# Softmax mixing and a cosine feed-forward layer on one core: the two correction products of the first product take bf16 operands

## The chip, the core and the metric

The kernel runs on one core of a Trainium2 chip. The core's engines run side by side and meet through semaphores: TensorE (PE in the profile; PEld is its weight loads), VectorE (DVE), ScalarE (ACT), GpSimd (POOL) and SyncE (SP), which issues the transfers. The metric is the device time of one launch in microseconds (us), as a median over runs.

## The reference

```python
# _attn_ref: x (8, 4096, 192), weight_gen (8, 4096, 8 heads, 7 taps)
w = weight_gen - np.max(weight_gen, axis=-1, keepdims=True)
w = np.exp(w)
w = w / (np.sum(w, axis=-1, keepdims=True) + 1e-09)
x_unf = x_pad[:, idx, :].reshape(B, S, K, H, group)     # each row and the 6 before it
out = np.einsum('bshk,bskhg->bshg', w, x_unf)
# _moe_ref: w_in (192, 2048), w_out (2048, 192)
h = x @ w_in
g = h * np.cos(h)
return (g @ w_out).astype(np.float32)
```

Each of the 32768 rows is first a softmax-weighted mix of itself and the six rows before it, for eight heads of 24 columns. The mixed rows go through a product with `w_in` (192 to 2048), the function h cos h, and a product with `w_out` (2048 to 192). The weights arrive as 64-bit floats.

## The kernel before, in words

**Blocks and periods.** The rows are cut into 64 blocks of 512 (4 rows on each of 128 partitions). A block passes the feed-forward layer in 8 periods, one for each pair of 128-column chunks of `w_in`. Period i works on block i // 8 and pair i % 8, so there are 512 periods, and 7 more to drain. The Python loop over i writes every engine's instructions in order, and a last pass ties each engine to this order; nothing reorders them but the hardware.

**The first product** is done three times in float32r (`F32R`, a shortened float32 on TensorE) so that it comes out nearly as float32: a value is split into a high part, rounded to float32r, and a low part, what the rounding left. With `w` and `x` split in this way, the kernel adds low x times high w, high x times low w, and high x times high w. The first two are the correction products. The 192 input columns don't fill 128 partitions evenly, so matmuls use 64 partitions each, two side by side on the halves of the array ("64*128" in the profile). `ffn_in_first` issues three such pairs of matmuls of 512 columns, `ffn_in_second` six: nine pairs a period, into the two PSUM banks of tile `h`, of which there are three in turn. `wa_*` and `wb_*` hold `w_in` (`wb_*` the middle 64 input columns); `x_hi` and `x_lo` hold the transposed rows of a block.

**Between the two parts** stands `ffn_out(j)` for j = i - 6, the second product: 16 matmuls of high g times `wo` (high and low part of `w_out` side by side, 384 columns, float32r), two small transposes of rows of a block two ahead into spare columns of the same PSUM tile `acc`, and 16 matmuls of low g times a bf16 copy `wo_b` (192 columns). A float32r matmul brings its weight load with it; a bf16 one has a separate LDWEIGHTS.

**The chain for h cos h** runs over ACT and DVE: turns (ACT, line 369: h rounded to whole turns), fraction (DVE, 379), cosine (ACT, 383), g (DVE, 386), high g (ACT, 393), low g (DVE, 397). ACT's order within a period is: turns of i - 1, high g of i - 2, cosine of i - 1, then in every second period the copy of `acc` to SBUF (`part`, 450) and in the others the copy of the transposed rows to `x_hi` (301). The first product of period i + 3 needs the PSUM tile that low g of i gives free.

**POOL** computes the mixing of a block ahead (lines 261 and 276), the sums of the second product's halves (466, 467) and `x_lo` (303) from `part` and `x_hi`. Once in 32 periods a softmax of four blocks runs; its exponential on ACT needs another function table than the cosine, so two table loads stand around it, and POOL has the sums and products of this softmax (185 to 226). In what follows, the stretch around it is called the softmax stretch.

**The start.** Weights are converted while the first periods run: ACT, three steps on DVE, a high copy on ACT, the low part on POOL (`two_parts`, lines 124 to 150). `two_parts` can also write a bf16 copy of the value (`half`), which before only `w_out_2` asks for. Blocks 0 to 3 are transposed whole, into an `h` tile; the others row by row in `ffn_out`.

Of the kernel before, what the change touches and what calls it, by code (L numbers as in the profile page):

```python
# [12 lines left out]
F32R = mybir.dt.float32r  # L13
I32 = mybir.dt.int32
U16 = mybir.dt.uint16
BF16 = mybir.dt.bfloat16
# [4 lines left out]
P = 128  # L21
# [22 lines left out]
def tile_softmax_conv_then_cos_ffn(  # L44
# [8 lines left out]
    nc = tc.nc  # L53
# [5 lines left out]
    F = w_in.shape[1]  # L59
# [4 lines left out]
    CT = R * P  # L64
# [12 lines left out]
    const = ctx.enter_context(tc.tile_pool(name="const", bufs=1))  # L77
    gpool = ctx.enter_context(tc.tile_pool(name="gpool", bufs=9))
    work = ctx.enter_context(tc.tile_pool(name="work", bufs=2))
# [3 lines left out]
    def h_banks(k):  # L83

        return ps_h.tile([P, 2, CT], F32, name="h", tag=f"h{k % 3}", bufs=1)
# [11 lines left out]


    wa_hi = const.tile([P, F], F32R, name="wa_hi")
    wa_lo = const.tile([P, F], F32R, name="wa_lo")  # L100

    wb_hi = const.tile([P, F // 2], F32R, name="wb_hi")
    wb_lo = const.tile([P, F // 2], F32R, name="wb_lo")
    wo = const.tile([P, NFC, 2 * D], F32R, name="wo")
    wo_b = const.tile([P, NFC, D], BF16, name="wo_b")

    def words(n, home="ghi"):

        if home == "ghi":
            raw = gpool.tile([P, 2 * CW], I32, name="raw", tag=home)  # L110
        elif home == "fin":
            raw = work.tile([P, R * D], I32, name="raw", tag=home)
        else:
            raw = work.tile([P, 2 * CT], I32, name="raw", tag=home)
        return raw[:, 0:2 * n]
# [8 lines left out]
    def two_parts(raw, hi, lo, half=None):  # L124
        shape = hi.shape[1:]
        n = math.prod(shape)

        def shaped(t, steps):
            t = t.rearrange("p (n s) -> p n s", s=steps)
            return t if len(shape) == 1 else t.rearrange("p (a b) s -> p a b s", b=shape[1])  # L130

        low, top = (shaped(raw, 2)[..., k] for k in range(2))
        size, bits = (shaped(t[:, 0:n], 1)[..., 0] for t in room.pop(0))
        nc.scalar.activation(out=size.bitcast(F32), in_=top.bitcast(F32), func=AF.Abs, scale=F64_SCALE)
        yield
        nc.vector.tensor_scalar(  # L136
            out=size, in0=size, scalar1=3, scalar2=None, op0=ALU.logical_shift_left)
        yield

        nc.vector.scalar_tensor_tensor(  # L140
            out=size, in0=top, scalar=-0x80000000, in1=size, op0=ALU.bitwise_and, op1=ALU.bitwise_or)
        yield

        nc.vector.scalar_tensor_tensor(  # L144
            out=bits, in0=low, scalar=29, in1=size, op0=ALU.logical_shift_right, op1=ALU.bitwise_or)
        yield
        nc.scalar.copy(out=hi, in_=bits.bitcast(F32))
        if half is not None:
            nc.scalar.copy(out=half, in_=bits.bitcast(F32))
        nc.gpsimd.tensor_tensor(out=lo, in0=bits.bitcast(F32), in1=hi.bitcast(F32), op=ALU.subtract)  # L150

    def w_in_a(c0, c1, home="ghi"):
        raw = words(c1 - c0, home)
        for n in range(2):
            nc.sync.dma_start(out=raw[n * D2:(n + 1) * D2],
                              in_=w_in[n * P:n * P + D2, c0:c1].bitcast(I32))
        return two_parts(raw, wa_hi[:, c0:c1], wa_lo[:, c0:c1])

    w_in_odd_even = w_in.rearrange("k (a n c) -> n k a c", n=2, c=P)

    def w_in_b(j):
        raw = words(CW)
        pairs = slice(j * CW // P, (j + 1) * CW // P)
        for n in range(2):
            nc.sync.dma_start(out=raw[n * D2:(n + 1) * D2].rearrange("k (a c) -> k a c", c=2 * P),
                              in_=w_in_odd_even[1 - n, D2:P, pairs, :].bitcast(I32))
        cols = slice(j * CW, (j + 1) * CW)
        return two_parts(raw, wb_hi[:, cols], wb_lo[:, cols])

    w_out_v = w_out.rearrange("(c p) d -> p c d", p=P)  # L170

# [111 lines left out]
    xT, transposed = {}, set()  # L283

    def traded(t):

        nc.sync.keepalive_nop([nc.sync.lower_ap(t)])
# [4 lines left out]
    def parts_of(b):  # L292
        if b not in xT:
            hi = work.tile([P, 2, CT], F32R, name="x_hi")
            lo = work.tile([P, 2, CT], F32R, name="x_lo")
            xT[b] = (hi, lo)
        return xT[b]

    def split(b, t, cs, eng):
        hi, lo = parts_of(b)  # L300
        nc.scalar.copy(out=hi[:, :, cs], in_=t)
        yield
        eng.tensor_tensor(
            out=lo[:, :, cs], in0=t, in1=hi[:, :, cs].bitcast(F32), op=ALU.subtract)

# [24 lines left out]
    def chunk(pair, n):  # L330
        return slice((2 * pair + n) * P, (2 * pair + n + 1) * P)

    def ffn_in_first(i, h=None):

        b, pair = divmod(i, NPAIR)
        x_hi, x_lo = xT[b]
        if h is None:
            h = h_banks(i)
        for m, (w, v) in enumerate(((wa_hi, x_lo), (wa_lo, x_hi), (wa_hi, x_hi))):
            for q in range(2):  # L340
                rs = slice(q * D2, (q + 1) * D2)
                nc.tensor.matmul(  # L342
                    h[:, q, :], lhsT=w[rs, chunk(pair, q)], rhs=v[rs, q, :],
                    start=(m == 0), stop=False, skip_group_check=True)
        hs[i] = h
        traded(h)

    def ffn_in_second(i):

        b, pair = divmod(i, NPAIR)  # L350
        x_hi, x_lo = xT[b]
        h = hs[i]
        prods = ((wa_hi, x_lo, 0), (wa_lo, x_hi, 0), (wb_hi, x_lo, 1), (wb_lo, x_hi, 1),
                 (wa_hi, x_hi, 0), (wb_hi, x_hi, 1))
        for m, (w, v, middle) in enumerate(prods):
            for q in range(2):
                rs = slice(q * D2, (q + 1) * D2)
                cs = slice(pair * P, (pair + 1) * P) if middle else chunk(pair, 1 - q)
                nc.tensor.matmul(  # L359
                    h[:, 1 - q, :], lhsT=w[rs, cs], rhs=v[rs, q ^ middle, :],  # L360
                    start=False, stop=(m == len(prods) - 1), skip_group_check=True)
# [77 lines left out]
    def evacuate(j):  # L439
# [9 lines left out]
        if WHOLE < bt < NB:  # L449
            nc.scalar.copy(out=part, in_=acc)  # L450
            r = group % R
            splits.append(split(bt, part[:, :, 2 * D:], slice(r * P, (r + 1) * P), nc.gpsimd))
        else:
            nc.scalar.copy(out=part[:, :, 0:2 * D], in_=acc[:, :, 0:2 * D])  # L454
# [70 lines left out]
    def all_of(*steps):  # L525
# [4 lines left out]

    late = [
        (-1, 1, w_in_a, (768, 1280)), (-1, 2, w_in_b, (1,)), (-1, 2, w_out_2, (0,)),
        (0, 3, w_in_a, (1280, 1792)), (0, 3, w_out_2, (1,)), (1, 4, w_out_2, (2, "part1")),
        (1, 4, w_out_2, (3, "part1")), (2, 5, w_in_a, (1792, 2048, "fin")),
        (2, 5, w_out_2, (4, "fin")), (4, 6, w_out_2, (5, "part1")), (4, 7, w_out_2, (6, "part1")),
        (5, 8, w_out_2, (7, "fin")),
# [19 lines left out]
    next(sm1)  # L556
    w_a0 = w_in_a(0, 256)
    w_b0 = w_in_b(0)
    load_rows(1)
    w_a1 = w_in_a(256, 768)  # L560
# [4 lines left out]
    def go_on(steps, n):  # L565
        for _ in range(n):
# [4 lines left out]
                      t=own_taps.rearrange("p (r h) k -> p r h k", h=H))  # L571
# [15 lines left out]
    go_on(w_a0, 3)  # L587
    go_on(w_b0, 3)
    first = split(0, tr, slice(0, CT), nc.vector)
    go_on(first, 1)  # L590
    all_of(w_a0, w_b0)
# [12 lines left out]
    for i in range(N + LAG + 1):  # L604
        b, pair = divmod(i, NPAIR)
# [22 lines left out]
        def products():  # L628
            if b < NB and pair == 0:
                assert b in transposed  # L630
            if whole is not None and j >= 0:

                ffn_out(j)
                ffn_in_first(i, whole)
            elif j >= N - HALF:
                if j == N - HALF:
                    last_half()
                return
            elif busy and EXP + 2 <= step <= EXP + 3:

                ffn_out(j, rest=False)
                ffn_in_first(i)
                ffn_out(j, rest=True)
            else:
                if i < N:
                    ffn_in_first(i, h_now if whole is None else whole)
                if j >= 0:
                    ffn_out(j)
            if i < N:
                ffn_in_second(i)  # L650
            if j in stores:
                stores.pop(j)()
            if j >= 0:
                evacuate(j)
# [15 lines left out]
        if whole is not None:  # L670
            t = work.tile([P, 2, CT], F32, name="part0", bufs=3)
            nc.scalar.copy(out=t, in_=whole)
            later.append(split(b + 1, t, slice(0, CT), nc.vector))
# [72 lines left out]
```

## Time and profile before

| what | value |
|---|---|
| median of 3 runs | 2257.45 us (2256.27 to 2257.81) |
| profiled execution, first to last instruction | 2256.1 us |
| PE busy | 2203.8 us (98%), 26496 matmuls |
| PE weight loads busy | 2009.9 us (89%) |
| DVE, ACT, POOL busy | 1922.0, 1886.0, 2001.4 us |
| mean granted TensorE clock | 0.993 |
| DMA | 47 GB/s on average |

The three runs lie 0.2 to 1.7 us above the profiled execution's span. The profile is one execution. "Busy" of PE counts from a matmul's start to its modelled end, so neighbours overlap, and the time that a matmul really holds the array is read from the distance between the starts of pairs. In a row of the timeline stand the start, the time covered, engine, line, operation, tile written and tiles read, count, and in brackets the idle time before it with the instruction that ended it. From about 150 us to 2200 us the periods repeat with 4.25 us, except in the softmax stretch.

### The profile page before, as it was taken

How to read it: one execution, taken by the hardware profiler on the slowest of the kernel's cores; microseconds unless marked ns; L12 is line 12 of the kernel's file. 1: busy time of each engine (PE TensorE's matmuls, PEld its weight loads, DVE VectorE, ACT ScalarE, POOL GpSimd, SP SyncE). 2: the span in 40 equal slices, each digit the busy share in tenths (PEclk: the TensorE clock that was granted, in tenths of full speed). 3: DMA queues.
4: the chain of work that ended last, by engine and by line, in shares of the span. 5: the costliest groups of instructions: out<-in, count | busy, mean ns of one | idle time of the engine just before them, and what ended most of it. 6: DMA issues, size and time to landing. Idle time of an engine off the chain costs nothing.

```text
span 2256.1 us, 60616 instructions
## 1 busy us (share of the span) xinstructions
PE 2203.8 (98%) x26496; PEld 2009.9 (89%) x26496; DVE 1922.0 (85%) x1663; ACT 1886.0 (84%) x2111; POOL 2001.4 (89%) x1460
## 2 busy tenths in 40 slices
PE   4899999999999999999999999999999999999998
PEld 2788889889999889999999988899999999899887
DVE  7888888888888888888888888888888888888887
ACT  4788888888888888888888888888888888888886
POOL 7999999998998989989998998989989899899941
PEclk8899999999999999999999999999999999999999
DMA  6221121121221221221211211211211211212100
GB/s 157 57 59 43 33 59 39 46 51 34 51 50 36 49 59 26 50 59 27 58 46 31 59 44 41 51 43 42 51 48 37 58 30 47 59 26 53 33 9 22
DMA packets 25767, 105.55 MB, mean 47 GB/s; under 512 B 2734, under 2 KB 6566, under 8 KB 25502
## 3 DMA queue, kind: packets, MB, share of 16 engines
q1 hardware_dynamic: 25502, 101.67, 18.4%
q8 instruction: 208, 3.41, 0.6%
q14 instruction: 57, 0.47, 0.1%
HBM read 76.50 MB, written 25.17 MB: 45 GB/s over the span
## 4 chain that ended last, share of the span: by engine, by line
PE 94%; DVE 2%; ACT 2%; POOL 1%; issue 1%; DMA 0%; SPq 0%; POOLq 0%; DVEq 0%; ACTq 0%
PE acc L427 45%; PE h L359 31%; PE h L342 16%; PE acc L321 1%; DVE glo L397 1%; ACT part L450 1%; ACT ghi L393 1%; POOL xa L276 1%; POOL pr L261 1%; PE h L491 0%; DVE turn L379 0%; DMA xt<-in_x_dram 0%; DVE h L140 0%; DVE h L136 0%; PE h L312 0%
## 5 line engine op out<-in xcount | busy, mean ns | idle before, releaser
L379 DVE TENSOR_TENSOR turn<-h,turn 128x1024 f32<-128x1024 f32 x512 | 625.5, 1222 | 281.2 <-ACT turn L369 281.2
L427 PE MATMUL acc<-wo,ghi 64*128 64x384 f32 x8112 | 807.2, 335 | 0.3 <-ACT part L454 0.3
L427 PEld LDWEIGHTS acc<-wo,ghi 64*128 64x128 f32 x8112 | 736.7, 185 | 35.9 <-ACT part L450 3.1
L276 POOL TENSOR_TENSOR xa<-xa,pr 128x768 f32<-128x768 f32 (+1 forms) x384 | 703.0, 1831 | 0.6
L383 ACT ACTIVATE turn<-turn 128x1024 f32<-128x1024 f32 x512 | 543.4, 1061 | 188.5 <-DVE turn L379 185.1
L386 DVE SCALAR_TENSOR_TENSOR h<-h,turn 128x1024 f32<-128x1024 f32 x512 | 631.0, 1233 | 20.3 <-ACT turn L383 20.3
L397 DVE TENSOR_TENSOR glo<-h,ghi 128x1024 bf16<-128x1024 f32 x512 | 622.5, 1216 | 2.7 <-ACT ghi L393 1.7
L369 ACT ACTIVATE turn<-h 128x1024 int32<-128x1024 f32 x497 | 510.2, 1027 | 125.5 <-PE h L359 118.6
L261 POOL TENSOR_TENSOR pr<-xt,taps 128x768 f32<-128x768 f32 (+1 forms) x384 | 589.5, 1536 | 11.9
L393 ACT CAST ghi<-h 128x1024 fp32r<-128x1024 f32 x512 | 518.0, 1012 | 14.2 <-DVE h L386 14.2
L427 PE MATMUL acc<-wo_b,glo 64*128 64x192 bf16 x8112 | 431.1, 243 | 0.0
L466 POOL TENSOR_TENSOR part<-part,part 128x768 f32<-128x768 f32 x126 | 234.3, 1859 | 157.2 <-ACT part L450 130.3
L427 PEld LDWEIGHTS <-glo 64*128 64x128 bf16 x8112 | 333.5, 94 | 23.0 <-issue 11.0
L359 PE MATMUL h<-x_lo,wa_hi 64*128 64x512 f32 x1024 | 253.0, 477 | 0.7
L450 ACT COPY part<-acc 128x1024 f32<-128x1024 f32 x240 | 239.6, 998 | 3.6 <-PE acc L427 3.6
L342 PE MATMUL h<-x_lo,wa_hi 64*128 64x512 f32 x1024 | 217.3, 407 | 20.5 <-DVE t L144 14.1
L359 PE MATMUL h<-x_lo,wb_hi 64*128 64x512 f32 x1024 | 211.8, 397 | 0.0
L342 PE MATMUL h<-x_hi,wa_lo 64*128 64x512 f32 x1024 | 210.1, 392 | 1.3 <-POOL wa_lo L150 1.3
L359 PE MATMUL h<-x_hi,wa_hi 64*128 64x512 f32 x1024 | 211.1, 395 | 0.0
L342 PE MATMUL h<-x_hi,wa_hi 64*128 64x512 f32 x1024 | 210.5, 393 | 0.0
L359 PE MATMUL h<-x_hi,wb_hi 64*128 64x512 f32 x1024 | 208.6, 390 | 0.0
L359 PE MATMUL h<-x_hi,wb_lo 64*128 64x512 f32 x1024 | 208.5, 390 | 0.0
(73 smaller groups left out, 2163.3 us busy)
## 6 DMA issues: line engine op xcount, KB each, us to landing
xt<-in_x_dram SPq DMA_DIRECT2D x62, 960.0 KB, 6.8
out_dram<-fin SPq DMA_DIRECT2D x63, 384.0 KB, 3.4
taps<-in_weight_gen_dram SPq DMA_DIRECT2D x15, 448.0 KB, 4.8
raw<-in_moe_w_out_dram SPq DMA_DIRECT2D x8, 384.0 KB, 4.2
raw<-in_moe_w_in_dram SPq DMA_DIRECT2D x10, 256.0 KB, 10.8
xt<-in_x_dram SPq DMA_DIRECT2D x1, 768.0 KB, 10.5
xt<-in_x_dram SPq DMA_DIRECT2D x1, 540.0 KB, 5.5
raw<-in_moe_w_in_dram SPq DMA_DIRECT2D x4, 128.0 KB, 4.6
```

Of the source, the lines that this page charges most:

```text
L261: eng.tensor_tensor(out=dst.rearrange("p r (h g) -> p r h g", h=H), in0=xt[:, k + ra:k + rb, :].rearrange("p r (h g) -> p r h g", h=H), in ...
L276: eng.tensor_tensor(out=acc if k < K else xa, in0=acc, in1=old[:, ra:rb], op=ALU.add)
L342: nc.tensor.matmul(h[:, q, :], lhsT=w[rs, chunk(pair, q)], rhs=v[rs, q, :], start=(m == 0), stop=False, skip_group_check=True)
L359: nc.tensor.matmul(h[:, 1 - q, :], lhsT=w[rs, cs], rhs=v[rs, q ^ middle, :], start=False, stop=(m == len(prods) - 1), skip_group_check=True)
L369: nc.scalar.activation(out=t.bitcast(I32), in_=hs[i], func=AF.Identity, bias=0.25, scale=1.0)
L379: nc.vector.tensor_tensor(out=t, in0=hs[i], in1=t.bitcast(I32), op=ALU.subtract)
L383: nc.scalar.activation(out=t, in_=t, func=AF.Sin, bias=SIN_BIAS, scale=SIN_SCALE)
L386: nc.vector.scalar_tensor_tensor(out=hs[i], in0=hs[i], scalar=TWO_PI, in1=turns.pop(i), op0=ALU.mult, op1=ALU.mult)
L393: nc.scalar.copy(out=hi, in_=hs[i])
L397: nc.vector.tensor_tensor(out=lo, in0=hs.pop(i), in1=hi.bitcast(F32), op=ALU.subtract)
L427: nc.tensor.matmul(to, lhsT=g[rs, n, t * P:(t + 1) * P], rhs=w[rs, fc, :], start=(lo == 0 and c == 0 and (whole or s == 0)), stop=(lo == 1 ...
L450: nc.scalar.copy(out=part, in_=acc)
```

## The change

Both low parts, `x_lo` and `wa_lo`/`wb_lo`, become bf16 tiles, and bf16 copies of the whole values are added: `x_b` of the transposed rows, `wa_b` and `wb_b` of `w_in`. The correction products then read bf16 on both sides: `x_lo` times `wa_b`, and `wa_lo` times `x_b`. The product of the high parts stays in float32r. The copies are made on ACT: `x_b` in `split`, behind the yield that follows `x_hi`, and `wa_b`/`wb_b` in `two_parts`. The tiles take as much SBUF as before.

```diff
-    wa_lo = const.tile([P, F], F32R, name="wa_lo")
+    wa_lo = const.tile([P, F], BF16, name="wa_lo")
+    wa_b = const.tile([P, F], BF16, name="wa_b")
-    wb_lo = const.tile([P, F // 2], F32R, name="wb_lo")
+    wb_lo = const.tile([P, F // 2], BF16, name="wb_lo")
+    wb_b = const.tile([P, F // 2], BF16, name="wb_b")
...
-        return two_parts(raw, wa_hi[:, c0:c1], wa_lo[:, c0:c1])
+        return two_parts(raw, wa_hi[:, c0:c1], wa_lo[:, c0:c1], wa_b[:, c0:c1])
...
-        return two_parts(raw, wb_hi[:, cols], wb_lo[:, cols])
+        return two_parts(raw, wb_hi[:, cols], wb_lo[:, cols], wb_b[:, cols])
...
     def parts_of(b):
         if b not in xT:
             hi = work.tile([P, 2, CT], F32R, name="x_hi")
-            lo = work.tile([P, 2, CT], F32R, name="x_lo")
-            xT[b] = (hi, lo)
+            half = work.tile([P, 2, CT], BF16, name="x_b")
+            lo = work.tile([P, 2, CT], BF16, name="x_lo")
+            xT[b] = (hi, half, lo)
...
     def split(b, t, cs, eng):
-        hi, lo = parts_of(b)
+        hi, half, lo = parts_of(b)
         nc.scalar.copy(out=hi[:, :, cs], in_=t)
         yield
+        nc.scalar.copy(out=half[:, :, cs], in_=t)
         eng.tensor_tensor(
             out=lo[:, :, cs], in0=t, in1=hi[:, :, cs].bitcast(F32), op=ALU.subtract)
...
-        for m, (w, v) in enumerate(((wa_hi, x_lo), (wa_lo, x_hi), (wa_hi, x_hi))):
+        for m, (w, v) in enumerate(((wa_b, x_lo), (wa_lo, x_b), (wa_hi, x_hi))):
...
-        prods = ((wa_hi, x_lo, 0), (wa_lo, x_hi, 0), (wb_hi, x_lo, 1), (wb_lo, x_hi, 1),
+        prods = ((wa_b, x_lo, 0), (wa_lo, x_b, 0), (wb_b, x_lo, 1), (wb_lo, x_b, 1),
                  (wa_hi, x_hi, 0), (wb_hi, x_hi, 1))
```

On PE, from the end of one period's second part through the next first part to the second product, there stood before:

```order
L359 MATMUL h<-x_hi,wa_hi 128x512 x2
L359 MATMUL h<-x_hi,wb_hi 128x512 x2
L342 MATMUL h<-x_lo,wa_hi 128x512 x2
L342 MATMUL h<-x_hi,wa_lo 128x512 x2
L342 MATMUL h<-x_hi,wa_hi 128x512 x2
L427 MATMUL acc<-wo,ghi 128x384 x16
```

and there stands now (lines are those of the changed file):

```order
L363 MATMUL h<-x_hi,wa_hi 128x512 x2
L363 MATMUL h<-x_hi,wb_hi 128x512 x2
L346 LDWEIGHTS wa_b
L346 MATMUL h<-x_lo,wa_b 128x512
L346 LDWEIGHTS wa_b
L346 MATMUL h<-x_lo,wa_b 128x512
L346 LDWEIGHTS wa_lo
L346 MATMUL h<-x_b,wa_lo 128x512
L346 LDWEIGHTS wa_lo
L346 MATMUL h<-x_b,wa_lo 128x512
L346 MATMUL h<-x_hi,wa_hi 128x512 x2
L431 MATMUL acc<-wo,ghi 128x384 x16
```

Two of the three pairs of the first part read bf16 and have loads of their own; in the second part it is four of six, and these four follow directly on the bf16 matmuls of the second product. No matmul changes its place.

On ACT, in the softmax stretch and the periods behind it, there stood before (`turn` stands for turns and cosine, `ghi` for high g):

```order
L301 CAST x_hi<-part_4583 128x2x128
L301 CAST x_hi<-part_4736 128x2x128
L369 ACTIVATE turn<-h 128x1024
L393 CAST ghi<-h 128x1024
L383 ACTIVATE turn<-turn 128x1024
L450 COPY part_4878<-acc 128x1024
L369 ACTIVATE turn<-h 128x1024
L393 CAST ghi<-h 128x1024
L383 ACTIVATE turn<-turn 128x1024
L301 CAST x_hi<-part_4878 128x2x128
L369 ACTIVATE turn<-h 128x1024
```

and there stands now:

```order
L304 CAST x_hi<-part_4625 128x2x128
L304 CAST x_hi<-part_4778 128x2x128
L306 CAST x_b<-part_4625 128x2x128
L306 CAST x_b<-part_4778 128x2x128
L373 ACTIVATE turn<-h 128x1024
L397 CAST ghi<-h 128x1024
L387 ACTIVATE turn<-turn 128x1024
L454 COPY part_4923<-acc 128x1024
L373 ACTIVATE turn<-h 128x1024
L397 CAST ghi<-h 128x1024
L387 ACTIVATE turn<-turn 128x1024
L304 CAST x_hi<-part_4923 128x2x128
```

Each copy to `x_hi` gets a second one to `x_b` behind it, ahead of the next period's turns; where two rows' copies had been put together, two are added. The order on DVE and POOL is the same as before.

On ACT at the start, from the transposed block 0 to the conversion of the third piece of `w_in` (line 134 is its first step), there stood before:

```order
L301 CAST x_hi<-h 128x1024
L147 CAST wa_hi<-t_173 128x256
L147 CAST wb_hi<-t_173 128x512
L134 ACTIVATE h<-raw 128x512
L147 CAST wa_hi<-t_207 128x512
```

and there stands now:

```order
L304 CAST x_hi<-h 128x1024
L149 CAST wa_hi<-t_175 128x256
L151 CAST wa_b<-t_175 128x256
L149 CAST wb_hi<-t_175 128x512
L151 CAST wb_b<-t_175 128x512
L306 CAST x_b<-h 128x1024
L136 ACTIVATE h<-raw 128x512
L149 CAST wa_hi<-t_213 128x512
```

Three copies now stand ahead of the conversion of the third piece.

More of the change, by code (lines that the diff above doesn't have):

```diff
@@ L335, in ffn_in_first @@
         b, pair = divmod(i, NPAIR)
-        x_hi, x_lo = xT[b]
+        x_hi, x_b, x_lo = xT[b]
         if h is None:
             h = h_banks(i)
-        for m, (w, v) in enumerate(((wa_hi, x_lo), (wa_lo, x_hi), (wa_hi, x_hi))):
+        for m, (w, v) in enumerate(((wa_b, x_lo), (wa_lo, x_b), (wa_hi, x_hi))):
             for q in range(2):
@@ L350, in ffn_in_second @@
         b, pair = divmod(i, NPAIR)
-        x_hi, x_lo = xT[b]
+        x_hi, x_b, x_lo = xT[b]
         h = hs[i]
-        prods = ((wa_hi, x_lo, 0), (wa_lo, x_hi, 0), (wb_hi, x_lo, 1), (wb_lo, x_hi, 1),
+        prods = ((wa_b, x_lo, 0), (wa_lo, x_b, 0), (wb_b, x_lo, 1), (wb_lo, x_b, 1),
                  (wa_hi, x_hi, 0), (wb_hi, x_hi, 1))
```

## The prediction

> **What bounds the kernel now.** I read the page's first and fourth part (who is busy, and which chain ended last), then the waits, then one period's timeline.
>
> ```profile
> PE 2203.8 (98%) x26496; PEld 2009.9 (89%) x26496; DVE 1922.0 (85%) x1663; ACT 1886.0 (84%) x2111; POOL 2001.4 (89%) x1460
> PE 94%; DVE 2%; ACT 2%; POOL 1%; issue 1%; DMA 0%; SPq 0%; POOLq 0%; DVEq 0%; ACTq 0%
> ACT turn L369 <- PE h L359: 118.6, 207, 1.3
> PE h L342 <- DVE glo L397: 1.7, 10, 0.3
> ```
>
> TensorE is on the last chain for 94% of the span and almost never waits; ACT waits for it in 207 of the periods. So a period lasts as long as its matmuls, and the question is how close the others follow. One period of PE:
>
> ```profile
> 1003.83 0.44 PE L342 MATMUL h<-x_lo,wa_hi 64*128 64x512 f32 x2
> ...
> 1004.53 1.61 PE L427 MATMUL acc<-wo,ghi 64*128 64x384 f32 x16
> 1005.94 0.26 PE L321 MATMUL acc<-ident,xa 64*128 64x64 f32 x2
> 1005.99 0.82 PE L427 MATMUL acc<-wo_b,glo 64*128 64x192 bf16 x15
> ...
> 1006.91 0.43 PE L359 MATMUL h<-x_hi,wa_lo 64*128 64x512 f32 x2
> ...
> 1007.85 0.43 PE L359 MATMUL h<-x_hi,wb_hi 64*128 64x512 f32 x2
> 1008.08 1.22 PE L427 MATMUL acc<-wo,ghi 64*128 64x384 f32 x11
> ```
>
> A float32r pair of 512 columns holds the array for 0.234 us: five from 1006.91 to 1008.08 (no first product follows here), and three from 1003.83 to 1004.53. The period: 3 x 0.234 + 1.41 (wo) + 0.05 (transposes) + 0.92 (wo_b and the second part's first pair) + 5 x 0.234 = 4.25 us.
>
> **The streams.** What a bf16 pair takes is read from `wo_b`, and the weight loads stand beside it:
>
> ```profile
> L427 PE MATMUL acc<-wo_b,glo 64*128 64x192 bf16 x8096 | 429.4, 243 | 0.0
> L427 PEld LDWEIGHTS acc<-wo,ghi 64*128 64x128 f32 x8096 | 734.0, 185 | 35.5 <-ACT part L450 3.1 <-POOL wo L150 0.7 <-issue 0.3
> L427 PEld LDWEIGHTS <-glo 64*128 64x128 bf16 x8096 | 332.3, 94 | 22.7 <-issue 10.7
> 37.92 0.63 PE L359 MATMUL h<-x_hi,wa_lo 64*128 64x512 f32 x2
> 39.63 0.63 PE L359 MATMUL h<-x_hi,wb_hi 64*128 64x512 f32 x2
> 37.50:40.00 2.50, 2.49 (x12) 1.64 (x12) 2.45 (x3) 2.39 (x4) 2.42 (x3) 0.55 0.56 176
> ```
>
> The 15 matmuls cover 0.82 us, the last alone 0.243, so seven pairs follow at 82.4 ns. By columns, 512 make 220 ns: the slow end. In the cold start (granted clock 0.55 in that window) a float32r pair takes (39.63 - 37.92) / 4 = 427 ns, so 512 columns need at least 213 at full clock: the fast end. I take 216, nearer to the fast end, as the 82.4 will hold a small fixed part. Six pairs save 6 x (234 - 216) = 108 ns, between 84 and 126. The seam behind `wo_b`: 8 x 82.4 = 659 ns of the 0.92 leaves 261 for the next pair, 27 over 234, since its load of 185 ns doesn't fit beside an 82 ns pair. Behind the change a bf16 load (94 ns) stands there: another 27 saved. There are now two places a period where float32r follows bf16, but behind pairs of 512 columns, which cover 185 ns; I cost them at nothing, at most 27 each. Together 135 ns, between 84 - 27 = 57 and 153; I take 130. A period comes to 4.12 us.
>
> **The copies on ACT.** Steady periods and the last copy's distance:
>
> ```profile
> 1016.84 0.99 ACT L450 COPY part<-acc 128x1024 f32<-128x1024 f32 x1
> 1017.73 1.03 ACT L369 ACTIVATE turn<-h 128x1024 int32<-128x1024 f32 x1
> ...
> 1020.05 1.06 ACT L383 ACTIVATE turn<-turn 128x1024 f32<-128x1024 f32 x1 [0.39 <-DVE turn L379]
> 1021.02 0.70 ACT L301 CAST x_hi<-part 128x256 fp32r<-128x256 f32 x2
> 1021.73 1.03 ACT L369 ACTIVATE turn<-h 128x1024 int32<-128x1024 f32 x1
> ...
> 1025.97 1.03 ACT L369 ACTIVATE turn<-h 128x1024 int32<-128x1024 f32 x1
> ...
> 1030.22 1.03 ACT L369 ACTIVATE turn<-h 128x1024 int32<-128x1024 f32 x1 [0.53 <-PE h L359]
> L301 ACT CAST x_hi<-part 128x256 fp32r<-128x256 f32 x240 | 92.2, 390 | 0.0
> L149 ACT CAST wo_b<-t 128x384 bf16<-128x384 f32 x8 | 4.1, 508 | 0.0
> L147 ACT CAST wo<-t 128x384 fp32r<-128x384 f32 x8 | 4.0, 502 | 0.0
> ```
>
> A bf16 output costs ACT what a float32r one does (508 against 502), so `x_b` is another `x_hi`: 390 ns alone, 0.70 - 0.39 = 0.31 behind its like. Turns to cosine takes 2.32 us, cosine to the next instruction 0.97: 3.29, which no other engine shortens. With `part` (0.89 from its start to the turns) a period needs 4.18, with `x_hi` 3.60, and with `x_b` 3.91, between 3.91 and 3.99. The mean of 4.18 and 3.91 is 4.045, under PE's 4.12, so ACT's 240 copies (74 us) lie in the idle time that now shows as 0.53 us in every second period. That cover shrinks to 4.12 x 2 - 8.09 = 0.15 us for two periods.
>
> **The softmax stretch.** Here ACT and POOL are late:
>
> ```profile
> 1136.39 1.03 ACT L369 ACTIVATE turn<-h 128x1024 int32<-128x1024 f32 x1
> ...
> 1157.58 0.70 ACT L301 CAST x_hi<-part 128x256 fp32r<-128x256 f32 x2
> 1158.31 1.03 ACT L369 ACTIVATE turn<-h 128x1024 int32<-128x1024 f32 x1
> 1143.33 0.74 POOL L303 TENSOR_TENSOR x_lo<-part,x_hi 128x256 fp32r<-128x256 f32 x1 [0.89 <-ACT x_hi L301]
> ...
> 1178.32 0.75 POOL L303 TENSOR_TENSOR x_lo<-part,x_hi 128x256 fp32r<-128x256 f32 x1
> 1143.33:1179.07 35.74, 35.59 (x429) 31.95 (x427) 32.69 (x29) 31.04 (x35) 35.02 (x29) 1.00 0.19 49
> 1179.32 0.42 PE L342 MATMUL h<-x_lo,wa_hi 64*128 64x512 f32 x2
> 1146.80:1283.38 136.58, 136.42 (x1664) 128.43 (x1665) 117.24 (x100) 116.87 (x131) 125.91 (x92) 1.00 0.18 45
> L303 POOL TENSOR_TENSOR x_lo<-part,x_hi 128x256 fp32r<-128x256 f32 x240 | 177.1, 741 | 30.5 <-ACT x_hi L301 30.3
> ```
>
> From the turns at 1136.39 the next ten periods lead to 1179.32, where PE starts the block whose last `x_lo` POOL finished at 1179.07. POOL got its start from ACT's `x_hi` behind the table loads and worked through: 35.02 of 35.74 us in 29 instructions, the rest small gaps. It can't be shortened by PE. Ten shorter periods would bring PE there 1.3 us earlier, 1.05 us ahead of POOL; of the 0.25 between them some 0.1 to 0.15 is the way of the signal. So this stretch keeps its 42.93 us but for 0.1. The two copies added at 1157.58 (0.62) delay turns that PE would find late, by less than the 1.05 that it has to wait for POOL anyway; I cost them at nothing, at most 0.6. The other 22 periods of a cycle save 0.13 each, 2.86 us. A cycle of 32 periods (the window's 136.58 us) comes to 133.62. POOL's 125.91 fits, if `x_lo` to bf16 still takes 741 ns; no row shows POOL writing bf16. Taking no change is nearest to ACT's pair of rows above; half and double are the bounds. The Trainium skill (GPSIMD Engine Reference, side-by-side cycle accounting) holds a two-input operation there to be bound by its shared read port, which would leave it unchanged; no run here shows it.
>
> **The start.** New ahead of the first conversions:
>
> ```profile
> 22.11 1.01 ACT L301 CAST x_hi<-h 128x1024 fp32r<-128x1024 f32 x1 [5.69 <-PE h L312]
> 23.02 0.41 ACT L147 CAST wa_hi<-t 128x256 fp32r<-128x256 f32 x1
> 23.53 0.62 ACT L147 CAST wb_hi<-t 128x512 fp32r<-128x512 f32 x1
> 24.05 0.63 ACT L134 ACTIVATE h<-raw 128x512 f32<-128x512 f32 x1
> ```
>
> `x_b` of a whole block costs 23.02 - 22.11 = 0.91 (four of them), a `wa_b`/`wb_b` piece of 512 columns 0.52 (five), one of 256 at most 0.41 (two): 7.1 us on ACT, all in the first 150. Three of them (1.74 us) delay the conversion at 24.05, the first whole-block copy also a first correction product; later ones stand beside DVE's conversions. Between 0 and 7.1 I take 2.5.
>
> **Sum.** 512 periods with a softmax stretch every 32 from period 29 on give 15 stretches and 14 whole cycles: 14 x 2.96 = 41.4. Behind the last stretch 24 periods, ahead of the first 7 regular ones: 31 x 0.13 = 4.0. The last stretch 0.1, the start -2.5: 43.0 saved, 2256.1 - 43.0 = 2213.1. The median stands 1.35 above this span: 2214.5 us.
>
> **The rivals.**
>
> *The pairs don't get faster* (the other side). For it: the 0.234 of float32r could come from 512 columns on two halves of the array, whatever the type; no row has 512 columns in bf16. Against it: `wo_b`'s 82.4 for 192, and the full-clock floor of 213. Then a period stays at 4.25, the start costs 2.5, and the two copies of a stretch, no longer behind a wait for POOL, cost up to 0.3 in each of 15, say 0.15: 2257.45 + 2.5 + 2.2 = 2262. It decides where a pair saves less than 4.7 us / (6 x 339 periods) = 2.3 ns. The Trainium skill (TensorE: Matmul & The Clock Gate, step 3, FILL) has throughput as purely N cycles and names no type, which would give both types the same time; the trace's 234 against 82.4 for 192 speaks against it for float32r. Chance 0.08.
>
> *ACT becomes the bound.* For it: a reserve of 0.15 us in two periods, and ACT comes out of the stretch late. Against it: `x_b` must take 4.12 x 2 - 4.18 - 3.60 = 0.46 before ACT's mean equals PE's, more than its 0.39 alone. If it came to 0.55, the period would be 4.165, a cycle would save 22 x 0.085 + 0.1 = 1.97, and the whole 14 x 1.97 + 2.6 - 2.5 = 27.7: 2230 us. Chance 0.16.
>
> *POOL doesn't hold the stretch*, because bf16 outputs are quicker or ACT passes the start on earlier. Then nearly all 32 periods save 0.13, less 0.3: 14 x 3.9 + 4 - 2.5 = 56: 2201 us. Against it: POOL's other rows in that run don't change. Chance 0.13.
>
> **How the numbers follow.** The forecast's case has 0.61, its own range is 2206 to 2226 (0.057 to 0.153 a period would give 2239 to 2207, the lower gain being unlikely as it needs every bound at once). 0.02 is left for what I don't see. The range 2198 to 2240 takes in the third rival and most of the second and leaves out the first. 0.2% is 4.5 us, about what a measurement of this kernel can tell from no change. Faster: 0.61 + 0.16 + 0.13 = 0.90, less 0.01; of the first rival's 0.08 half lies within 0.2%, half beyond; with the rest, same 0.05 and slower 0.06.
>
> **What the profile after would show.** Pairs on bf16 at 0.216 from start to start, and no 27 ns behind `wo_b`; regular periods of 4.12; `x_b` at 390 ns, with ACT's wait for PE down from 118.6 us to some 30; in the softmax stretch the block's first matmul tied to POOL's `x_lo`, with the cycle at 133.6. I would be wrong if float32r behind bf16 costs a drain of its own, if `x_lo` takes longer than 741 ns on POOL (16 in a cycle, 7.7 us to spare, so 0.48 us each), or if the late ACT holds PE beyond the stretch.

## The result, and the profile after

The changed kernel takes 2220.53 us (median of 4 runs, 2219.9 to 2220.93) against 2257.02 before; the ratio is 0.9836, with a 95% interval of 0.9822 to 0.985. It is faster by 36.5 us, 6.0 us less than forecast, and lies in the forecast's own range (2206 to 2226). The profiled span fell by 37.3 us, from 2256.1 to 2218.8. The parts of the page that answer to those shown of before, and then the waits:

```profile
PE 2156.4 (97%) x26496; PEld 1673.8 (75%) x26496; DVE 1921.1 (87%) x1663; ACT 1946.4 (88%) x2362; POOL 1996.1 (90%) x1460
...
PE 70%; DVE 14%; ACT 11%; issue 3%; POOL 2%; DMA 0%; ACTq 0%; SPq 0%; DVEq 0%; POOLq 0%
```

```profile
PEld L346 <- DVE glo L401: 28.5, 63, 1.3
...
PEld acc L431 <- ACT part L454: 23.7, 60, 0.4
...
ACT turn L373 <- PE h L363: 11.0, 13, 2.4
```

The last chain now runs a quarter over DVE and ACT (14% and 11%, before 2% each), ACT hardly waits for PE (11.0 us, before 118.6, where some 30 were forecast), and PE's loads wait for low g in 63 places and for the copy `part` in 60 (columns: us in total, number of waits, the longest). The waits of 0.4 us for `part` were not in the forecast. And the sign that was to tell of POOL, the first matmul of the stretch's block tied to POOL's `x_lo`, is not there: no wait of PE for it is listed. A regular period of PE:

```profile
1036.85 0.39 PE L346 MATMUL h<-x_lo,wa_b 64*128 64x512 bf16 x2
1037.08 0.38 PE L346 MATMUL h<-x_b,wa_lo 64*128 64x512 bf16 x2
1037.11 0.58 PE L346 MATMUL h<-x_hi,wa_hi 64*128 64x512 f32 x2
1037.53 1.57 PE L431 MATMUL acc<-wo,ghi 64*128 64x384 f32 x16
1038.94 0.22 PE L325 MATMUL acc<-ident,xa 64*128 64x64 f32 x2
1038.99 0.82 PE L431 MATMUL acc<-wo_b,glo 64*128 64x192 bf16 x16
1039.65 0.38 PE L363 MATMUL h<-x_lo,wa_b 64*128 64x512 bf16 x2
1039.87 0.38 PE L363 MATMUL h<-x_b,wa_lo 64*128 64x512 bf16 x2
1040.08 0.38 PE L363 MATMUL h<-x_lo,wb_b 64*128 64x512 bf16 x2
1040.30 0.38 PE L363 MATMUL h<-x_b,wb_lo 64*128 64x512 bf16 x2
1040.33 0.58 PE L363 MATMUL h<-x_hi,wa_hi 64*128 64x512 f32 x2
1040.75 0.40 PE L363 MATMUL h<-x_hi,wb_hi 64*128 64x512 f32 x2
1040.99 0.39 PE L346 MATMUL h<-x_lo,wa_b 64*128 64x512 bf16 x2
```

From 1039.65 to 1040.30 three bf16 pairs take 0.65 us, 0.217 each (215.8 ns as a mean over the trace's records). The Trainium skill (TensorE: Matmul & The Clock Gate, Back-to-back issue gap) gives N / 2.4 + 2.5 ns for an isolated gap, which is 216 for 512 columns, and some 131 for a long stream. The bf16 pairs of this stream agree with the first; the float32r pairs, 233 ns, follow neither. `wo_b` takes 0.66 us (1038.99 to 1039.65) and nothing is lost behind it. From the last bf16 pair to the second float32r pair it is 1040.30 to 1040.75, 0.45 us, which is one pair of each kind: float32r behind bf16 costs nothing that shows here. But the first bf16 pair behind float32r, 1036.85 to 1037.08, takes 0.23 (226 ns by the records), 10 more than its like. The period is 4.133 us, 113 ns less than the 4.247 before (means over the regular periods of both traces), where 130 were forecast.

Where the 37.3 us came from, by the starts of periods and blocks in both traces:

| place | forecast | measured |
|---|---|---|
| to period 22 | -2.5 | -0.96 |
| periods 22 to 28, the last included | 0.9 | -0.18 |
| 14 cycles | 14 x 2.96 = 41.4 | 14 x 2.52 = 35.27 |
| last softmax stretch | 0.1 | 0.53 |
| 24 periods behind it | 3.1 | 2.60 |
| sum | 43.0 | 37.3 |

One cycle (stretch from the turns of period 253 to the first matmul of period 264; the cycle counted from period 256 to 288) is 134.03 us, before 136.58. Of the 2.55 saved, the stretch has 0.26 (42.66, before 42.92), and the other 22 periods have 22 x 0.113 = 2.49 less 0.2, since one of them, period 252, takes 4.33. So three sizes were off in a cycle: the regular period, period 252, and what the stretch gives. The windows of the cycle and the stretch (columns as in the prediction's window rows: length, then busy time and count of PE, PEld, DVE, ACT, POOL, then granted clock, DMA share, GB/s):

```profile
1130.27:1264.31 134.04, 133.62 (x1666) 103.95 (x1666) 117.12 (x100) 120.46 (x147) 125.60 (x92) 1.00 0.19 46
1119.97:1162.63 42.66, 42.23 (x521) 32.12 (x518) 37.21 (x33) 39.07 (x48) 40.87 (x33) 1.00 0.19 45
```

POOL is busy for 125.60 us (125.91 before), ACT for 3.59 more than before (116.87). The two groups whose price the forecast had to assume:

```profile
L307 POOL TENSOR_TENSOR x_lo<-part,x_hi 128x256 bf16<-128x256 f32 x240 | 176.8, 740 | 29.2 <-ACT x_hi L304 29.2
...
L306 ACT CAST x_b<-part 128x256 bf16<-128x256 f32 (+1 forms) x243 | 97.9, 409 | 0.0
```

POOL writes bf16 in 740 ns, float32r took 741. `x_b` without its three whole-block copies (1.01 us each) is (97.9 - 3.0) / 240 = 395 ns.

### The profile page after: what moved, and what is told of

It is laid out like the page before. It is cut to its first block, busy times and chain, and to the rows that moved or that the text cites. A ratio compares the mean times of both kernels' runs of the same rounds, so it can differ in the third digit from the quotient of the medians.

```text
span 2218.8 us, 60657 instructions
## 1 busy us (share of the span) xinstructions
PE 2156.4 (97%) x26496; PEld 1673.8 (75%) x26496; DVE 1921.1 (87%) x1663; ACT 1946.4 (88%) x2362; POOL 1996.1 (90%) x1460
## 4 chain that ended last, share of the span: by engine, by line
PE 70%; DVE 14%; ACT 11%; issue 3%; POOL 2%; DMA 0%; ACTq 0%; SPq 0%; DVEq 0%; POOLq 0%
PE acc L431 35%; PE h L363 22%; PE h L346 11%; DVE turn L383 6%; DVE glo L401 3%; ACT turn L373 3%; ACT part L454 3%; DVE h L390 2%; ACT turn L387 1%; ACT ghi L397 1%; PE acc L325 1%; ACT L387 1%; ACT L211 1%; DVE top L206 1%; ACT x_hi L304 1%
## 5 line engine op out<-in xcount | busy, mean ns | idle before, releaser
L431 PEld LDWEIGHTS acc<-wo,ghi 64*128 64x128 f32 x8112 | 726.8, 185 | 53.9 <-ACT part L454 23.7
L431 PE MATMUL acc<-wo_b,glo 64*128 64x192 bf16 x8112 | 425.1, 243 | 0.0
L431 PEld LDWEIGHTS <-glo 64*128 64x128 bf16 x8112 | 327.3, 94 | 27.5 <-issue 10.6
L363 PE MATMUL h<-x_hi,wa_hi 64*128 64x512 f32 x1024 | 300.8, 582 | 0.0
L346 PE MATMUL h<-x_hi,wa_hi 64*128 64x512 f32 x1024 | 299.3, 580 | 0.0
L346 PE MATMUL h<-x_lo,wa_b 64*128 64x512 bf16 x1024 | 201.1, 388 | 29.4 <-DVE t L146 14.7
L363 PE MATMUL h<-x_hi,wb_hi 64*128 64x512 f32 x1024 | 204.0, 394 | 0.0
L307 POOL TENSOR_TENSOR x_lo<-part,x_hi 128x256 bf16<-128x256 f32 x240 | 176.8, 740 | 29.2 <-ACT x_hi L304 29.2
L346 PE MATMUL h<-x_b,wa_lo 64*128 64x512 bf16 x1024 | 196.4, 379 | 1.7 <-POOL wa_lo L152 1.7
L363 PE MATMUL h<-x_lo,wa_b 64*128 64x512 bf16 x1024 | 196.1, 378 | 0.7
L363 PE MATMUL h<-x_b,wa_lo 64*128 64x512 bf16 x1024 | 196.3, 378 | 0.0
```

Source lines behind the costliest of these rows:

```text
L346: nc.tensor.matmul(h[:, q, :], lhsT=w[rs, chunk(pair, q)], rhs=v[rs, q, :], start=(m == 0), stop=False, skip_group_check=True)
L363: nc.tensor.matmul(h[:, 1 - q, :], lhsT=w[rs, cs], rhs=v[rs, q ^ middle, :], start=False, stop=(m == len(prods) - 1), skip_group_check=True)
L431: nc.tensor.matmul(to, lhsT=g[rs, n, t * P:(t + 1) * P], rhs=w[rs, fc, :], start=(lo == 0 and c == 0 and (whole or s == 0)), stop=(lo == 1 ...
```

## The experiments

The theory going in: the matmuls gain what the period shows, the copies on ACT cost nothing in regular periods, and POOL's `x_lo` holds the softmax stretch. The rival: ACT, late by its two added copies, holds it.

**1. The copies alone.** The kernel before, with all of the change's copies made on ACT into a spare tile that nothing reads; all matmuls stay float32r:

```diff
+    spare = const.tile([P, 2, CT], BF16, name="spare")
+    spare_w = spare.rearrange("p a b -> p (a b)")
-        return two_parts(raw, wa_hi[:, c0:c1], wa_lo[:, c0:c1])
+        return two_parts(raw, wa_hi[:, c0:c1], wa_lo[:, c0:c1], spare_w[:, 0:c1 - c0])
...
         yield
+        nc.scalar.copy(out=spare[:, :, cs], in_=t)
```

> The kernel before with the added copies on ACT alone, in the same places, written to a spare tile that nothing reads; all matmuls stay float32r. If regular periods have room for them (0.53 us idle on ACT in every second one), these stay at 4.245 us. Theory ACT: the two copies together make the turns behind the stretch 0.6 us late, of which the slack of 0.6 us between low g and the next first product takes most: 0 to 0.5 us a cycle, with 1 to 2.5 us at the start 2258 to 2267 us. Theory POOL: POOL's x_lo has 0.25 us to spare and doesn't move, so only the start shows: 2258 to 2260 us.

Measured: 2265.88 us, ratio 1.0036 (1.0023 to 1.0048). The timeline of PE at the end of a regular period:

```profile
1043.46 0.41 PE L363 MATMUL h<-x_hi,wa_hi 64*128 64x512 f32 x2
1043.69 0.41 PE L363 MATMUL h<-x_hi,wb_hi 64*128 64x512 f32 x2
1043.92 0.41 PE L346 MATMUL h<-x_lo,wa_hi 64*128 64x512 f32 x2
1044.15 0.41 PE L346 MATMUL h<-x_hi,wa_lo 64*128 64x512 f32 x2
1044.39 0.40 PE L346 MATMUL h<-x_hi,wa_hi 64*128 64x512 f32 x2
```

Four pairs take 0.93 us and the period 4.247, both as before, so the copies cost a regular period nothing, and the gain of the change is that of the matmuls. The span grew by 6.8 us: 4.25 of it lie ahead of period 29, and 14 cycles cost 0.17 each, 2.4. In a cycle it is the stretch that grows, from 42.92 to 43.11, while POOL's `x_lo` ends 42.66 behind the turns, before 42.68: ACT's lateness alone delays PE there, a first sign for the rival. The start is thus dearer than the 2.5 forecast; in the changed kernel this is hidden by what some 29 early periods gain. What comes late there, in the changed kernel (ACT, DVE, then PE), with the first matmul of before in a fence of its own:

```profile
22.35 1.01 ACT L304 CAST x_hi<-h 128x1024 fp32r<-128x1024 f32 x1 [5.68 <-PE h L316]
...
24.91 1.01 ACT L306 CAST x_b<-h 128x1024 bf16<-128x1024 f32 x1
25.82 0.64 ACT L136 ACTIVATE h<-raw 128x512 f32<-128x512 f32 x1
25.96 1.23 DVE L307 TENSOR_TENSOR x_lo<-h,x_hi 128x1024 bf16<-128x1024 f32 x1 [2.21 <-ACT x_b L306]
27.23 0.61 PE L346 MATMUL h<-x_lo,wa_b 64*128 64x512 bf16 x2 [4.92 <-DVE x_lo L307]
```

```profile
24.78 0.79 PE L342 MATMUL h<-x_lo,wa_hi 64*128 64x512 f32 x2 [2.71 <-ACT h L134]
```

The first matmul comes 2.45 us later. It needs `x_lo`, and DVE's `x_lo` starts only when ACT's whole-block copy to `x_b` has ended (24.91 + 1.01 = 25.92), 2.54 us later than before (23.42), although it doesn't read `x_b`. Both read the transposed block in the PSUM tile `h`; the next whole blocks are read from `part` in SBUF, and there `x_lo` starts while the copy runs (74.25, with the copy from 74.12 to 75.17). The start follows the end of the copy by 0.03 us in this trace and in experiment 1's; why it is tied to it is not shown. Without `x_b` (experiment 2) the first matmul stands at 24.80, so the copies of the weights cost nothing up to there.

**2. Without `x_b`.** `x_lo` stands in for `x_b`, so that the product of low w with high x is left out (low w is multiplied by low x in its place) and the 244 copies to `x_b` (243 from `part`, one from `h`) fall away; the matmuls keep their number, type and order:

```diff
-            half = work.tile([P, 2, CT], BF16, name="x_b")
-        nc.scalar.copy(out=half[:, :, cs], in_=t)
-        x_hi, x_b, x_lo = xT[b]
+        x_hi, x_lo = xT[b]
+        x_b = x_lo
```

> Without the copies x_b, the second correction product reads x_lo in their place: the product of high x and low w is left out, every matmul keeps its type, size and place. It asks what the 244 copies on ACT cost. In the changed kernel a cycle of 32 periods takes 134.04 us: 32 regular periods of 4.132 would be 132.2, so 1.8 us are lost in the softmax stretch and at period 28. Theory ACT (the copies make ACT late there): a cycle falls to about 32 x 4.132 + 0.74 (the loss of the kernel before) = 133.0, some 15 us in 14 cycles, and the start gains 1 to 2: about 2204 us. Theory POOL (the ten periods of the stretch are held by POOL's x_lo, which ends 42.57 us behind the turns at the stretch's start): the stretch keeps 42.6 us, only the 0.2 us at period 28 go: about 2216 us. Under both, regular periods stay at 4.13 us.

Measured: 2216.04 us (2215.84 to 2216.44), ratio 0.9816 (0.9803 to 0.9829). Its waits and the first matmul of the stretch's last block:

```profile
PE h L345 <- POOL x_lo L305: 3.7, 14, 0.5
```

```profile
1158.83 0.39 PE L345 MATMUL h<-x_lo,wa_b 64*128 64x512 bf16 x2 [0.25 <-POOL x_lo L305]
```

This is what the theory of POOL expects: PE, no longer slowed by ACT, comes to the block earlier and waits for `x_lo`, once in each of 14 stretches. The stretch is 42.58, 0.08 less. All copies to `x_b` cost 4.5 us; 3.1 of them lie ahead of period 29 (173.94 against 177.05). That the total, 2216, was hit is partly luck: the start gave 3.1 where 1 to 2 were expected, and the 0.2 us of period 252 (28 in the first cycle), which were expected to go, stayed.

**3. `x_b` early.** The copy to `x_b` moves within the changed kernel to the place between high g and cosine, one period later, where ACT waits for DVE's fraction anyway:

```diff
+    halves = []
-        nc.scalar.copy(out=half[:, :, cs], in_=t)
+        if eng is nc.gpsimd:
+            halves.append(lambda: nc.scalar.copy(out=half[:, :, cs], in_=t))
+        else:
+            nc.scalar.copy(out=half[:, :, cs], in_=t)
...
             act_hi(i - 2)
+        if halves:
+            halves.pop(0)()
```

> The same work as the changed kernel, but each row's copy x_b is issued one period later, between high g and the cosine, where ACT waits 0.39 us for DVE; of two rows put together one goes into each of two periods. Theory ACT: the 0.31 us of a copy vanish in that wait, the turns behind the stretch come 0.6 us earlier, and a cycle falls by 0.8 to 1.0 us: about 2207 us. Theory POOL: the stretch keeps 42.6 us, and only the 0.2 us at period 28 go: about 2217 us. If ACT's wait for DVE only moves, the time stays at 2220.

Measured: 2219.26 us (2219.19 to 2219.58), ratio 0.983 (0.9817 to 0.9844). The waits, and the same place as in experiment 2:

```profile
PE h L351 <- POOL x_lo L312: 1.9, 9, 0.4
```

```profile
1161.65 0.39 PE L351 MATMUL h<-x_lo,wa_b 64*128 64x512 bf16 x2 [0.18 <-POOL x_lo L312]
```

ACT is freed: from the turns of period 253 to those of 258 it takes 21.80 us instead of 22.39. But PE then waits for POOL, and the stretch is 42.60, shorter by 0.06 only. The time lies between what was expected with the theory of POOL (2217, with period 252 mended, which again takes 4.34) and no change.

**4. The mixing later.** Two products of a later block's mixing, which stand ahead of this `x_lo` on POOL, move behind it, so that `x_lo` is finished 3 us earlier:

```diff
-        for _ in range(3 if 5 <= i < 20 or i < 64 and i % 4 == 0 else 2):
+        light = i >= 64 and step == 13 and b + 4 < NB
+        for _ in range(3 if 5 <= i < 20 or i < 64 and i % 4 == 0 else 0 if light else 2):
```

> The changed kernel with the two first products of the next block's mixing moved behind x_lo on POOL in the one period of the softmax stretch in which they stood ahead of the last x_lo, which so ends about 3.05 us earlier; they are made up for in the following periods, behind the mixing that is due. In the changed kernel two limits coincide, if the last runs are read rightly: PE comes by ACT's pace 0.10 us behind x_lo, and POOL alone would allow 0.05. Then POOL's relief is worth at most 0.05 x 14 = 0.7 us: 2220 us, the stretch 42.6 us, x_lo some 3 us ahead. If POOL alone held the stretch, it would fall by 0.4 us or more, to 2214.

Measured: 2220.31 us (2219.78 to 2221.26), ratio 0.9835 (0.9822 to 0.9849). POOL's `x_lo` and the matmul that reads it, first in the changed kernel:

```profile
1161.80 0.73 POOL L307 TENSOR_TENSOR x_lo<-part,x_hi 128x256 bf16<-128x256 f32 x1
...
1162.63 0.39 PE L346 MATMUL h<-x_lo,wa_b 64*128 64x512 bf16 x2
```

and with the mixing later:

```profile
1159.08 0.73 POOL L307 TENSOR_TENSOR x_lo<-part,x_hi 128x256 bf16<-128x256 f32 x1
...
1162.95 0.39 PE L346 MATMUL h<-x_lo,wa_b 64*128 64x512 bf16 x2
```

In the changed kernel `x_lo` is done at 1162.53 and PE comes 0.10 us later; where PE waits for `x_lo` (experiments 2 and 3) it starts 0.05 behind its end. With the mixing later `x_lo` is done at 1159.81 and PE comes 3.14 us later, at its own time: the stretch stays at 42.67. So in the changed kernel POOL doesn't hold it.

**5. Both.** `x_b` early and the mixing later together.

> The copies x_b issued early (between high g and the cosine) and the two products moved behind x_lo, together. Alone, the first was worth 1.3 us (against the changed kernel's 2220.5) and the second at most 0.7, by the reading that both limits stand at the same place. Then both together free what the early copies showed as a wait of 0.34 us ahead of the block: a stretch of about 42.25 us, 14 x 0.35 = 5 us: 2214 us. If POOL was not what PE waited for, the sum of the two stays under 2 us: 2218 to 2219.

Measured: 2215.27 us (2214.99 to 2215.74), ratio 0.9813 (0.9799 to 0.9826). One alone gives 1.3 us, the other 0.2, which is no difference (the kernel before differs by 0.5 between the measurements), both 5.3. The cycles say the same: 134.03 in the changed kernel, 133.97 and 134.05 with one, 133.67 with both, and the stretch falls to 42.27. ACT's lateness and POOL's `x_lo` were two limits at the same place, within 0.1 us of each other.

**6. Less on POOL, in the wrong place.** One of two mixing steps is left to a later period in three periods of the stretch, to lighten POOL:

```diff
-        for _ in range(3 if 5 <= i < 20 or i < 64 and i % 4 == 0 else 2):
+        light = busy and i >= 64 and EXP + 2 <= step <= EXP + 4
+        for _ in range(3 if 5 <= i < 20 or i < 64 and i % 4 == 0 else 1 if light else 2):
```

> The changed kernel with one step of the mixing less on POOL in each of three periods of the softmax stretch, made up for later, so that x_lo of the stretch's block ends about 4 us earlier. Theory POOL: the stretch is no longer held at 42.6 us and falls to what ACT allows. Theory ACT: PE reaches the block 0.1 us behind x_lo by its own pace already, so nothing moves: 2220 us, with the stretch at 42.67 us and x_lo some 4 us ahead of its first matmul.

Measured: 2266.32 us (2264.91 to 2267.87), ratio 1.0038 (1.0026 to 1.0051). The mixing that was put off is due itself, for the two transposes of the next rows:

```profile
PEld acc L325 <- POOL xa L278: 39.7, 14, 2.9
```

```profile
1179.97 0.28 PE L325 MATMUL acc<-ident,xa 64*128 64x64 f32 x2 [2.60 <-POOL xa L278]
```

It tells nothing between the theories: three steps put off make PE wait for 2.6 us at another place. Experiment 4 moves steps of a later block for that reason.

**7. The seams.** In the second part each float32r pair goes right behind its two bf16 pairs, so that a period has one more change from float32r to bf16:

```diff
-        prods = ((wa_b, x_lo, 0), (wa_lo, x_b, 0), (wb_b, x_lo, 1), (wb_lo, x_b, 1),
-                  (wa_hi, x_hi, 0), (wb_hi, x_hi, 1))
+        prods = ((wa_b, x_lo, 0), (wa_lo, x_b, 0), (wa_hi, x_hi, 0), (wb_b, x_lo, 1),
+                  (wb_lo, x_b, 1), (wb_hi, x_hi, 1))
```

> The changed kernel with the six pairs of the second part in another order: bf16, bf16, float32r, bf16, bf16, float32r, so that a period has one more change from bf16 to float32r and one more back. By the prediction's step (a change behind pairs of 512 columns costs nothing) a period stays at 4.132 and the time at 2220 us. By its bound (27 ns each) a period takes 0.054 more: 27 us, 2247. By the trace of the changed kernel, where the pair behind float32r starts 7 ns late and the next one 10 and the change to float32r shows nothing, one more change back costs 17 ns: 512 x 0.017 = 8.7 us, 2229 us, period 4.149.

Measured: 2223.24 us (2223.15 to 2223.49), ratio 0.9848 (0.9835 to 0.9861). The new seam:

```profile
1040.52 0.38 PE L363 MATMUL h<-x_b,wa_lo 64*128 64x512 bf16 x2
1040.55 0.58 PE L363 MATMUL h<-x_hi,wa_hi 64*128 64x512 f32 x2
1040.97 0.39 PE L363 MATMUL h<-x_lo,wb_b 64*128 64x512 bf16 x2
1041.20 0.38 PE L363 MATMUL h<-x_b,wb_lo 64*128 64x512 bf16 x2
```

1040.52 to 1040.97 is again 0.45, one pair of each kind; the bf16 pair behind it takes 0.23. The period grows by 7 ns, to 4.140, and the kernel by 2.7 us; none of the three expected values (4.132, 4.149, or 0.054 more) was met. The seam costs neither nothing nor 27 ns: the bf16 pair that follows float32r takes 10 ns more (226 by the records), and the two float32r pairs, no longer next to each other, give some of it back.

**8. The maximum in halves.** Period 252 takes 4.33 us in the changed kernel, and also without `x_b`. DVE, ACT and PE's loads there:

```profile
1107.78 1.07 DVE L206 TENSOR_REDUCE top<-taps 128x128 f32<-128x896 f32 x1
1108.78 1.21 DVE L383 TENSOR_TENSOR turn<-h,turn 128x1024 f32<-128x1024 f32 x1
...
1110.02 1.06 ACT L387 ACTIVATE turn<-turn 128x1024 f32<-128x1024 f32 x1 [0.77 <-DVE turn L383]
1110.99 1.00 ACT L454 COPY part<-acc 128x1024 f32<-128x1024 f32 x1
...
1112.04 1.34 PEld L431 LDWEIGHTS acc<-wo,ghi 64*128 64x128 f32 x16 [0.36 <-ACT part L454]
```

The softmax's maximum stands ahead of the fraction on DVE, cosine waits 0.77 us for the fraction instead of 0.39, `part` comes late, and the second product waits for the `acc` that `part` reads. The edit cuts the reduction in two, one half in each of two periods:

```diff
-        nc.vector.tensor_reduce(out=top, in_=t, axis=AX.X, op=ALU.max)
+        m = n if early else n // 2
+        nc.vector.tensor_reduce(out=top[:, 0:m], in_=t[:, 0:m], axis=AX.X, op=ALU.max)
         yield
+        if m < n:
+            nc.vector.tensor_reduce(out=top[:, m:n], in_=t[:, m:n], axis=AX.X, op=ALU.max)
```

> The changed kernel, but the maximum reduction of each softmax (1.08 us on DVE) is cut into two halves, one in each of two successive periods; nothing else moves. In the changed kernel the fourth period after it starts (period 252) takes 4.33 us instead of 4.13, and the turns of period 251 stand 0.47 us behind PE. If the reduction delays the fraction and so the copy to part, and the second product waits for that copy, a half of 0.55 us fits nearly into the 0.47 us that DVE has free in a period: period 252 comes to 4.13 to 4.17, a cycle to 133.85, and 14 to 15 softmaxes save 2.2 to 2.9 us: 2217.9 us. If something else in that period makes the 0.2 us, period 252 stays at 4.33 and the time at 2220.5.

Measured: 2217.18 us (2216.27 to 2217.6), ratio 0.9822 (0.9809 to 0.9836). DVE and ACT at the same place:

```profile
1106.04 0.61 DVE L207 TENSOR_REDUCE top<-taps 128x64 f32<-128x448 f32 x1
1106.63 1.23 DVE L386 TENSOR_TENSOR turn<-h,turn 128x1024 f32<-128x1024 f32 x1
...
1107.89 1.06 ACT L390 ACTIVATE turn<-turn 128x1024 f32<-128x1024 f32 x1 [0.39 <-DVE turn L386]
```

Cosine waits 0.39 as everywhere, period 252 is 4.13 and the cycle 133.84. The cause of the 0.2 us is shown, and it is worth 3.3 us by the medians, 3.0 by the profiled spans.

**9. All three.** Experiments 5 and 8 together.

> The early x_b copy, the later mixing and the halved maximum reduction together. If the 0.2 us of period 252 are separate from the softmax stretch, the gains add: 2215.3 less 2.6 is 2212.7 us, with a cycle of 133.48. If what is saved ahead of the stretch is waited for in it again, 2215.3.

Measured: 2211.97 us (2211.8 to 2212.17), ratio 0.98 (0.9787 to 0.9813), the best version: 45.1 us under the kernel before. The cycle:

```profile
1125.64:1259.08 133.44, 132.85 (x1666) 104.15 (x1666) 117.33 (x101) 120.55 (x147) 125.40 (x92) 1.00 0.19 46
```

The gains add.

## Why the prediction was right, and where its sizes were off

- **The pairs:** right for bf16. 216 ns was taken and 215.8 came; the 27 ns behind `wo_b` are gone; float32r behind bf16 costs nothing that shows. The floor of 213 is half of 427 and so needs a clock of 0.50; the row shown has 0.55 as the mean of a longer window, and 37.92 to 39.63 alone has 0.50.
- **The period:** the mis-sized term. "I take 130" became 113. A float32r pair was read as 234 ns from one place; over the regular periods of before it is 232.5 (0.93 us for four in experiment 1), so a bf16 pair saves 16.7 and not 18: 6 x 16.7 is 100, where 108 was taken. And the forecast priced the seams at which float32r follows bf16 and not the one at which bf16 follows float32r: 10 ns (the period after, and experiment 7). 100 + 27 - 10 makes 117; the 4 that are left are not taken apart by any run. Over 339 periods the 17 ns are 5.8 us.
- **The copies on ACT:** right for regular periods. 395 ns against 390, and experiment 1 leaves the period at 4.247. The cover of 0.15 us for two periods was thin, as computed, but it held.
- **Period 252:** missing. The forecast asked how close ACT and POOL follow in a shorter period, and not DVE. Where DVE has one more thing to do, the softmax's maximum, the shorter period leaves no room: period 252 lost 0.2 us in every cycle, 14 x 0.2 = 2.8. It isn't the copies' doing, as it takes 4.33 without `x_b` too. In the kernel before the same reduction left the turns 0.17 us late and PE didn't notice (4.24).
- **The softmax stretch:** near in time, wrong in part of its cause, and so in part luck. It was to keep its length but for 0.1, and kept it but for 0.26. POOL's `x_lo` ends 42.56 us behind the turns, before 42.68, so POOL indeed can't be shortened much; but the way from `x_lo` to PE, estimated at 0.1 to 0.15, is 0.05, so the most that POOL left to gain was 0.3. And "the two copies ... I cost them at nothing" holds only because two limits coincide: the copies make the turns 0.59 us later (22.39 against 21.80), and that lateness, not POOL, sets the changed kernel's stretch (experiment 4). Without the copies it would be POOL's `x_lo`, 0.06 to 0.08 earlier (experiments 2 and 3). With both removed 0.39 a cycle are gained (experiment 5).
- **`x_lo` on POOL:** right, 740 ns against 741. The Trainium skill (GPSIMD Engine Reference, side-by-side cycle accounting) binds a two-input operation to its read port; an unchanged time with a narrower output agrees.
- **The start:** -0.96 to period 22 against -2.5, by two errors that offset each other. The copies cost 3.8 us up to there (experiment 1), more than was taken, within the bound of 7.1, and most of that is `x_lo` of block 0 behind its `x_b`, 2.45 us at the first matmul; the forecast gave the periods ahead of 22 no gain, and they have one. Periods 22 to 28, taken for regular, are not: period 23, behind the last whole-block copies, takes 4.75 us (4.72 in experiment 1, 4.25 before), and period 28 takes 4.34.
- **The rivals:** that the pairs don't get faster fell by 215.8 against 232.5. That ACT becomes the bound happened in the stretch only (by 0.06 to 0.08 us), not in the regular period, which is 4.13 with `x_b` and without. That POOL doesn't hold the stretch is true, but ACT stood in the same place, so the further 13 us that this rival saw didn't come.

## What to carry to other kernels

When a change shortens the engine that bounds, price both directions of every seam between operand types, and look for the periods that are not regular: there the cover of the next engines, ample on the mean, is used up first. Where an experiment that lifts one limit gains nothing, lift the suspected second one together with it before calling either harmless: here 1.3 us and nothing clear of noise apart made 5.3 together. A cost that is hidden by a gain at the same place (the start) is found only by making the cost without the gain.

## What the hardware showed that was not expected

A bf16 pair of 512 columns takes 226 ns behind a float32r pair and 216 behind its like, while a float32r pair behind a bf16 pair of that length pays nothing that shows; one more of both seams a period costs 7 ns in all. And the move to bf16 unloads the weight loads more than the matmuls: PE's loads were busy for 2009.9 us and now for 1673.8, against 2203.8 and 2156.4 of the matmuls.
